# Whole float32 key sums and numerators, and third tiles in the room they leave

## The chip, the cores and the metric

The program runs on one core of a Trainium2 chip. Time is device time of one execution in microseconds (us). The kernel before took 961.89 us in the median of three runs (961.02 to 962.08). A core has five engines: TensorE multiplies matrices (PE in the profile; PEld is its weight load), VectorE (DVE), ScalarE (ACT) and GpSimd (POOL) work on elements, and SyncE (SP) issues most DMAs. Each has its own queue and works through it in order; they meet by semaphores. TensorE writes to PSUM, from which VectorE and ScalarE read.

## The reference

Three layers follow each other. In numpy, with what matters here:

```
def phi(x):                                    # x: q or k, scaled; [4, 8, 576, 64]
    h = einsum(x, omega) - sum(x*x)/2          # 128 features
    return exp(h - max(h)) / sqrt(128)
kv  = einsum('bhsm,bhsd->bhmd', k_p, v);  z = sum(k_p, axis=2)        # key sums
num = einsum('bhsm,bhmd->bhsd', q_p, kv); den = einsum('bhsm,bhm->bhs', q_p, z) + 1e-6
x = (num / den) as [2304, 512]
x = softplus(x @ w_in) @ w_out                 # w_in [512, 2048], w_out [2048, 512], given as float64
x = expert layer: one of 8 experts for each token by cosine, relu(x @ w1[e]) @ w2[e] times its gate
```

The key sums `kv` and `z` are sums over the 576 positions of products of key features and values; a column of ones beside the 64 columns of `v` gives `z` from the same product.

## The kernel before, in words

**Two forms of product.** A matrix product here is either whole, with both operands in float32, or split: each operand is a part rounded to the float32r type (`hi`) and the remainder (`lo`), and hi·hi, hi·lo and lo·hi are summed in PSUM. A split product is three matmuls, and somebody has to make the parts: a cast (VectorE, ScalarE or GpSimd) and a subtraction (VectorE or GpSimd).

**Attention.** The work is cut by batch `b` (4) and head quadruple `u` (2 for each batch; called a head pair below, since each holds two pairs of heads `i`). For each, keys come in four full tiles `w` = (i, half) of 128 partitions x 2 heads x 2 rows, and one short tile `"rem"` for the last 64 positions; queries alike. One tile is an item, and an item is a chain of stages that sit in numbered steps: transpose at step t (`stage_T`), features at t+1 (`stage_P`: products, maximum, exponential), for keys the splitting at t+3 (`stage_S`, with `split_v` for the value tile) and the key sum at t+4 (`stage_K`, on PSUM bank `kv`), then `stage_Z`, which transposes the sums into `kzh` (and the remainder `kzl`). Query features are transposed at t+3 (`stage_Q`, into `qT..hi` and `qT..lo`), and `stage_N` makes numerator and denominator, 256 or 320 columns each. `f_k` and `f_n` in TUNE say for which of the eight head pairs a form is whole: key sums of the full tiles for the first three (`11100000`), numerators for the first four (`11110000`). Short key tiles are split everywhere. A whole key tile needs its values beside a column of ones in float32, so `split_v` copies them (L249) into such a tile and GpSimd sets the ones (L284).

**Loads.** SP loads key, query and value tiles four steps ahead of the item. `raw` and `rawv` have two buffers each, so a load waits for the reader of the tile two before.

**Feed-forward layer.** 2304 tokens are six groups `g` of 384, and the 2048 hidden features 16 chunks `f`; `n` = 16 g + f counts chunks. For a chunk `mm1` makes `h` (one PSUM bank in groups 0 to 3), ScalarE and VectorE make softplus from it (`r` and `t`, L690 to L711), `act_tail` splits it into `gh` and `gl` (L717 to L720), and `mm2` sums into three PSUM banks. `mm1` of chunk n+2 is issued before `mm2` of chunk n. `r`, `gh` and `gl` have two tiles, `t` one. In group 0 all products are whole, later ones split, with weights split anew for each chunk (`ring_in`, `ring_out`).

**Weights.** The two weight matrices come as float64. `load_w` brings a piece of 512 KB as pairs of integers into a staging tile (`wst`, two of them), and `conv_ops` makes float32 of it in three VectorE instructions (L601, L604, L607). `conv_all` loads piece n+1 and then converts piece n; there are 32 pieces.

**What sets the order.** The program emits 30 steps of the attention, then the chunks; between the products of a chunk `attn_point` emits attention stages and one instruction of the conversion by a budget, and a table `need` says which step has to be done before a group starts. The framework then lays out the instructions anew: at build time a planner simulates the engines with costs of its own and takes, on each engine, what is ready first by its reckoning, with the order of emission as priority. The order on the chip is the one that it left, fixed in each engine's queue. Only the expert layer, from its second unit on, keeps a written order.

**Memory.** The attention's tiles lie in pools `ac`, `ap` and `ap1`, which are closed during group 4; the feed-forward layer's lie in `fp`, `ring`, `xpool`, `stg`. A tile of a pool is given out again when its readers are done.

Of the kernel before, what the change touches and what calls it, by code (L numbers as in the profile page):

```python
# [23 lines left out]
    f_k='11100000',  # L24
    f_n='11110000',
# [6 lines left out]
    vf='vvvvvvvv',  # L32
    exp_k='vaaavaaa',
    exp_q='vavvaavv',
    kh='vavvavav',
    kl='ppppvvvv',
    vh='vpvvvvpv',
    vl='ppvppppp',
# [16 lines left out]
    s_lag=3,  # L55
    k_lag=4,
    q_lag=3,
    setup=2,
# [6 lines left out]
    order='XSMTNnKPZ',  # L65
    se={'T': 't', 'Q': '12', 'P': 'p0', 'N0': 'h', 'N1': '12'},
    sl={'T': 't', 'Q': 't', 'P': 'p', 'N0': 't', 'N1': 't'},
    b_vh=3,
# [7 lines left out]
    b_rawv=2,  # L76
# [7 lines left out]
def tile_kernel(ctx, tc, q, k, v, omega, w_in, w_out, emb, tau, w1, w2, out):  # L84
# [94 lines left out]
    raw = {}  # L179

    def load_half(kind, b, j, half):
        src = {"q": q, "k": k, "v": v}[kind]
        nb = TUNE["b_rawv" if kind == "v" else "b_raw"]
        t = atile([P, 2, 2, D], F32, "rawv" if kind == "v" else "raw", b, nb)
        s = src[b, 2 * j:2 * j + 2, 0:S0, :].rearrange("h (p r) d -> p h r d", r=4)
        nc.sync.dma_start(out=t, in_=s[:, :, 2 * half:2 * half + 2, :])
        raw[kind, b, j, half] = t

    def load_rem(kind, b, u):
        src = {"q": q, "k": k, "v": v}[kind]  # L190
        t = ap.tile([P, 2, D], F32, tag="rem", bufs=TUNE["b_rem"], name=f"rem_{kind}_{b}_{u}")
        for i in range(2):
            j = 2 * u + i
            nc.sync.dma_start(
                out=t[SR * i:SR * i + SR],
                in_=src[b, 2 * j:2 * j + 2, S0:S, :].rearrange("h p d -> p h d"))
        raw[kind, b, u, "rem"] = t
# [4 lines left out]
    vhi = [ac.tile([P, 2, 2, D + 1], F32R, name=f"vhi{i}") for i in range(TUNE["b_vh"])]  # L202

    vhr = [ac.tile([P, 2, D + 1], F32R, name=f"vhr{i}") for i in range(2)]
    vlr = [ac.tile([P, 2, D], F32R, name=f"vlr{i}") for i in range(2)]

    def setup():
        obd = stg.tile([P, 2, M], F32, tag="wst", name="obd")
        nc.gpsimd.memset(obd, 0.0)
        for t in vhi:  # L210
            nc.gpsimd.memset(t[:, :, :, D:D + 1].bitcast(F32), 1.0)
        for i in range(2):
            nc.gpsimd.memset(vhr[i].bitcast(F32), 0.0)
            nc.gpsimd.memset(vlr[i].bitcast(F32), 0.0)
            nc.gpsimd.memset(vhr[i][SR * i:SR * i + SR, :, D:D + 1].bitcast(F32), 1.0)
        pt = psum("T", "om_ps")
        nc.tensor.transpose(pt[:, 0:P], om2.rearrange("m j d -> m (j d)"), ident)
        for j in range(2):
            r = slice(64 * j, 64 * j + 64)
            nc.scalar.activation(out=obd[r, j, :], in_=pt[r, 0:P], func=AF.Copy, scale=SC)  # L220
        nc.gpsimd.tensor_copy(obd_hi, obd)
        nc.gpsimd.tensor_tensor(out=obd_lo, in0=obd, in1=obd_hi.bitcast(F32), op=ALU.subtract)
# [14 lines left out]
    def cols(w):  # L237
        return 1 if w == "rem" else 2
# [30 lines left out]
    nv, nk = [0], [0]  # L269

    def split_v(it):
        b, u, kind, w = it
        if w == "rem":
            vr = raw["v", b, u, "rem"]
            for i in range(2):
                r = slice(SR * i, SR * i + SR)
                nc.vector.tensor_copy(vhr[i][r, :, 0:D], vr[r])
                nc.gpsimd.tensor_tensor(out=vlr[i][r], in0=vr[r], in1=vhr[i][r, :, 0:D].bitcast(F32),
                                        op=ALU.subtract)
        else:  # L280
            vr = raw["v", b, 2 * u + w[0], w[1]]
            if kind == "k" and whole("k", b, u):
                vf = atile([P, 2, 2, D + 1], F32, "vl", b)
                nc.gpsimd.memset(vf[:, :, :, D:D + 1], 1.0)  # L284
                move("vf", b, u, vf[:, :, :, 0:D], vr)
                st["v", b, 2 * u + w[0], w[1]] = (vf, None)
                return
            vh = vhi[nv[0] % len(vhi)]
            nv[0] += 1
            vl = atile([P, 2, 2, D], F32R, "vl", b)  # L290
            eng("vh", b, u).tensor_copy(vh[:, :, :, 0:D], vr)
            eng("vl", b, u).tensor_tensor(out=vl, in0=vr, in1=vh[:, :, :, 0:D].bitcast(F32), op=ALU.subtract)
            st["v", b, 2 * u + w[0], w[1]] = (vh, vl)

    def stage_P(it):
# [14 lines left out]
        if kind == "k" and w != "rem" and whole("k", b, u):  # L310
            nk[0] += 1
            pe = atile([P, 4, M], F32, ("kh", "kl")[nk[0] % 2], b)
        else:
            pe = atile([P, 4, M], F32, "pe", b, TUNE["b_pe"])
# [10 lines left out]
    def stage_S(it):  # L325
        b, u, kind, w = it
        n = cols(w)
        pe = st.pop((it, "P"))
        split_v(it)
        if kind == "k" and w != "rem" and whole("k", b, u):  # L330
            st[it, "P"] = (pe, None)
        elif kind == "k":
            kh = atile([P, 4, M], F32R, "kh", b)
            kl = atile([P, 4, M], F32R, "kl", b)
            if TUNE["kh"][2 * b + u] == "a":
                nc.scalar.copy(out=kh[:, :2 * n], in_=pe[:, :2 * n])
            else:
                eng("kh", b, u).tensor_copy(kh[:, :2 * n], pe[:, :2 * n])
            eng("kl", b, u).tensor_tensor(out=kl[:, :2 * n], in0=pe[:, :2 * n],
                                          in1=kh[:, :2 * n].bitcast(F32), op=ALU.subtract)  # L340
            st[it, "P"] = (kh, kl)

    def stage_K(it):
        b, u, kind, w = it
        kh, kl = st.pop((it, "P"))
        if w == (0, 0):
            st["kv", b, u] = psum("kv", "kv")
        kv = st["kv", b, u]
        if w == "rem":
            lst = [(i, h, vhr[i][:, h, :], vlr[i][:, h, :], h) for i in range(2) for h in range(2)]  # L350
        else:
            vh, vl = st.pop(("v", b, 2 * u + w[0], w[1]))
            lst = [(w[0], h, vh[:, h, r, :], None if vl is None else vl[:, h, r, :], 2 * h + r)
                   for r in range(2) for h in range(2)]
        for n, (i, h, a_hi, a_lo, c) in enumerate(lst):
            col = (2 * i + h) * M
            first = w == (0, 0) and n == 0
            o = kv[0:D + 1, col:col + M]
            if kl is None:
                nc.tensor.matmul(o, lhsT=a_hi, rhs=kh[:, c, :], start=first, stop=False, skip_group_check=True)  # L360
                continue
            nc.tensor.matmul(o, lhsT=a_hi, rhs=kh[:, c, :], start=first, stop=False, skip_group_check=True)
            nc.tensor.matmul(o, lhsT=a_hi, rhs=kl[:, c, :], start=False, stop=False, skip_group_check=True)
            nc.tensor.matmul(kv[0:D, col:col + M], lhsT=a_lo, rhs=kh[:, c, :], start=False,
                             stop=(w == "rem"), skip_group_check=True)
        if w == "rem":
            kvs = ap1.tile([D + 1, 512], F32, tag="kvs", name="kvs")
            move("kvs", b, u, kvs, kv[0:D + 1, :])
            st["kvs", b, u] = kvs
# [131 lines left out]
    def add_item(t, it):  # L501
        b, u, kind, w = it
        tl = max(0, t - AHEAD)
        for kd in ("k", "v") if kind == "k" else ("q",):
            if w == "rem":
                loads[tl].append(lambda kd=kd: load_rem(kd, b, u))
            else:
                loads[tl].append(lambda kd=kd: load_half(kd, b, 2 * u + w[0], w[1]))
        steps[t].append(("T", 214, lambda: stage_T(it)))
        steps[t + 1].append(("P", 654, lambda: stage_P(it)))  # L510
        if kind == "k":
            steps[t + TUNE["s_lag"]].append(("S", 0, lambda: stage_S(it)))
            steps[t + TUNE["k_lag"]].append(("K", 648, lambda: stage_K(it)))
            if w == "rem":
                steps[t + TUNE["k_lag"] + 1].append(("Z", 216, lambda: stage_Z(b, u)))
        else:
            steps[t + TUNE["q_lag"]].append(("K", 428, lambda: stage_Q(it)))
# [57 lines left out]
    def load_w(n):  # L575
        f, which = divmod(n, 2)
        t = stg.tile([P, 2 * DM], I32, tag="wst", name="wst")
# [36 lines left out]
    def conv_all():  # L614
        load_w(0)
        for n in range(NW):
            if n + 1 < NW:
                load_w(n + 1)
            yield from conv_ops(n)
            done_w[0] = n + 1  # L620
# [35 lines left out]

    def mm1(n, rate):
# [20 lines left out]

        if two:
            r = fp.tile([P, G], F32, tag="r", name="r")  # L680
# [7 lines left out]
        t = fp.tile([P, G], F32, tag="t", name="t", bufs=1)  # L688
        r = fp.tile([P, G], F32, tag="r", name="r")
# [11 lines left out]
    def act_tail(n):  # L701
        r, t = gt[n]
        if n < NF:
            gf = fp.tile([P, G], F32, tag="gh", name="gf")
# [9 lines left out]
        gh = fp.tile([P, G], F32R, tag="gh", name="gh")  # L714
        gl = fp.tile([P, G], F32R, tag="gl", name="gl")
# [911 lines left out]
```

## Time and profile before

| | us |
|---|---|
| median of the runs (range) | 961.89 (961.02 to 962.08) |
| profiled execution | 964.16 |
| its span, first to last instruction | 962.4 |
| PE busy | 898.1 (93%) |
| DVE busy | 745.9 (78%) |
| ACT busy | 655.6 (68%) |
| POOL busy | 365.4 (38%) |
| mean granted TensorE clock | 0.991 |

The profile shows one execution. Busy time of an engine is the time covered by at least one of its instructions; matmuls overlap, since each is shown with its latency, so the distance from one start to the next tells what a matmul holds the engine for. A name before `<-` is the tile written, the names behind it are read; L303 is a line of the kernel. The first feed-forward product starts at 75.7 us, group 1 at 194.8, group 2 at 309.5, group 3 at 411.7, group 4 at 502.2; the last key sum is at 422.8 and the last numerator at 489.6; the expert layer's products run from 642.6 to 947.9.

### The profile page before, as it was taken

What the parts mean: (1) busy time and instruction counts of PE and PEld (TensorE: products, weight loads), DVE (VectorE), ACT (ScalarE), POOL (GpSimd) and SP (SyncE); (2) the same over time, 40 slices, a digit from 0 to 9 for tenths busy, and PEclk for the clock granted to TensorE, in tenths of its full rate; (3) what the DMA queues carried; (4) which work ended last, traced back from release to release, by engine and by line L of the source; (5) the groups of instructions that cost most, each with busy time, mean ns of one, the idle gap of its engine ahead of it and who ended that gap; (6) DMA issues with size and microseconds to landing.
All of it is one profiled execution on the core that took longest, in us unless ns stands there. A gap on an engine that the chain in (4) does not pass through costs nothing. (4 is left out here: it accounts for less than half of the span.)

```text
span 962.4 us, 15065 instructions
## 1 busy us (share of the span) xinstructions
PE 898.1 (93%) x5095; PEld 744.4 (77%) x5095; DVE 745.9 (78%) x1497; ACT 655.6 (68%) x1463; POOL 365.4 (38%) x396
## 2 busy tenths in 40 slices
PE   7788998999997989999999999999999999999994
PEld 6666554587887978898878899887787888878873
DVE  7999788478997789989997677768976675675762
ACT  4887434477766976777767778777866576585672
POOL 2436302165653676468663210011252252241410
PEclk9999999999999999999999999999999999999997
DMA  5554354011252114011210174101122761551810
GB/s 147 163 150 131 118 188 146 12 31 45 55 125 60 45 36 119 9 35 35 46 26 17 34 269 169 34 12 41 26 78 102 306 234 34 204 185 60 339 65 7
DMA packets 77840, 94.73 MB, mean 98 GB/s; under 512 B 33398, under 2 KB 66166, under 8 KB 75456
## 3 DMA queue, kind: packets, MB, share of 16 engines
q1 hardware_dynamic: 69184, 45.21, 17.7%
q0 software_dynamic: 8576, 48.52, 13.4%
q8 instruction: 42, 0.69, 0.3%
q14 instruction: 38, 0.31, 0.1%
HBM read 108.36 MB, written 15.48 MB: 129 GB/s over the span
## 5 line engine op out<-in xcount | busy, mean ns | idle before, releaser
L1407 PE MATMUL po<-w,mh_h 128*128 128x512 f32 x368 | 116.8, 398 | 0.5 <-ACT mh_h L1384 0.5
L740 PE MATMUL y<-woh,gh 128*128 128x512 f32 x240 | 96.3, 410 | 8.1 <-DVE gh L719 7.6
L1287 DVE TENSOR_TENSOR w<-w2r,w 128x512 fp32r<-128x512 f32 x136 | 88.2, 684 | 14.1 <-ACT w L1283 13.9
L1422 POOL DMA_INDIRECT out_dram<-ot,s_idx x23 | 31.1, 1352 | 170.1 <-ACT ot L1421 139.8
L740 PE MATMUL y<-wol,gh 128*128 128x512 f32 x240 | 93.4, 397 | 0.0
L1283 ACT CAST w<-w2r 128x512 fp32r<-128x512 f32 x136 | 79.4, 643 | 20.6 <-DMA w2r<-in_moe_w_dram,w_idx 7.1
L1287 DVE TENSOR_TENSOR w<-w1r,w 128x1024 fp32r<-128x1024 f32 x68 | 80.4, 1225 | 11.2 <-ACT w L1283 11.1
L640 DVE TENSOR_TENSOR wil<-win,wih 128x512 fp32r<-128x512 f32 x72 | 63.3, 879 | 24.9 <-ACT wih L639 24.5
L740 PE MATMUL y<-woh,gl 128*128 128x512 f32 x240 | 79.4, 400 | 0.0
L1407 PEld LDWEIGHTS po<-w,mh_h 128*128 128x128 f32 x368 | 66.1, 189 | 12.2 <-ACT mh_h L1384 0.7
L1283 ACT CAST w<-w1r 128x1024 fp32r<-128x1024 f32 x68 | 72.0, 1119 | 3.4 <-PE ph L1373 2.1
L1395 PE MATMUL ph<-mxh,w 128*128 128x256 f32 x384 | 73.0, 286 | 1.3 <-DVE w L1287 0.5
L674 PE MATMUL h<-xhi,wih 128*128 128x384 f32 x320 | 72.6, 347 | 1.5 <-DVE t L694 1.3
L1407 PE MATMUL po<-w,mh_l 128*128 128x512 f32 x184 | 72.7, 395 | 0.7 <-DVE mh_l L1386 0.7
L674 PE MATMUL h<-xlo,wih 128*128 128x384 f32 x320 | 69.7, 336 | 0.0
L674 PE MATMUL h<-xhi,wil 128*128 128x384 f32 x320 | 69.7, 337 | 0.0
L652 POOL TENSOR_TENSOR wol<-wout,woh 128x512 fp32r<-128x512 f32 x40 | 58.4, 1460 | 25.7 <-ACT woh L651 18.3
L1395 PEld LDWEIGHTS ph<-mxh,w 128*128 128x128 f32 x384 | 62.7, 195 | 5.1 <-DVE w L1287 3.7
L674 PEld LDWEIGHTS h<-xhi,wih 128*128 128x128 f32 x320 | 55.4, 188 | 6.6 <-DVE t L694 1.8
L740 PEld LDWEIGHTS y<-woh,gh 128*128 128x128 f32 x240 | 45.0, 189 | 18.6 <-DVE gh L719 9.3
L674 PEld LDWEIGHTS h<-xhi,wil 128*128 128x128 f32 x320 | 57.4, 188 | 0.0
L1260 POOL DMA_INDIRECT w1r<-in_moe_w_dram,w_idx x17 | 22.5, 1324 | 91.2 <-issue 55.8
(346 smaller groups left out, 2588.9 us busy)
## 6 DMA issues: line engine op xcount, KB each, us to landing
wst<-in_moe_w_in_dram SPq DMA_DIRECT2D x16, 512.0 KB, 3.9
wst<-in_moe_w_out_dram SPq DMA_DIRECT2D x16, 512.0 KB, 3.6
raw<-in_k_dram SPq DMA_DIRECT2D x32, 128.0 KB, 2.4
rawv<-in_v_dram SPq DMA_DIRECT2D x32, 128.0 KB, 2.3
raw<-in_q_dram SPq DMA_DIRECT2D x32, 128.0 KB, 2.2
ya<-yt SPq DMA_DIRECT2D x20, 128.2 KB, 4.9
yb<-yt SPq DMA_DIRECT2D x20, 128.2 KB, 3.7
ya<-yt SPq DMA_DIRECT2D x8, 256.5 KB, 5.0
```

Source lines behind the costliest of these rows:

```text
L640: feng("il", n).tensor_tensor(out=il, in0=wi, in1=ih.bitcast(F32), op=ALU.subtract)
L652: feng("ol", n).tensor_tensor(out=ol, in0=wo, in1=oh.bitcast(F32), op=ALU.subtract)
L674: nc.tensor.matmul(h[:, 0:G], lhsT=a[:, c, :], rhs=x[:, c, :], start=(i == 0), stop=(i == last))
L740: nc.tensor.matmul(y, lhsT=x[:, c], rhs=w, start=(f == 0 and i == 0), stop=(f == NF - 1 and i == len(passes) - 1))
L1260: nc.gpsimd.indirect_dma_start(out=raw_w[nm, s % 2], out_offset=None, in_=src, in_offset=bass.IndirectOffsetOnAxis(ap=w_idx[:, s:s + 1].bi ...
L1283: nc.scalar.copy(out=hi, in_=src)
L1287: eng.tensor_tensor(out=lo, in0=src, in1=hi.bitcast(F32), op=ALU.subtract)
L1395: nc.tensor.matmul(ph[:, j * 256:j * 256 + 256], lhsT=w1s[g, c][b_][:, f], rhs=xs[g][a][c].rearrange("p i t -> p (i t)"), start=(c == 0 an ...
L1407: nc.tensor.matmul(po[s], lhsT=h[a][:, o:o + P], rhs=w2s[g, c][b_], start=(c == 0 and n == 0), stop=(c == 7 and n == 2))
L1422: nc.gpsimd.indirect_dma_start(out=out, out_offset=bass.IndirectOffsetOnAxis(ap=s_idx[:, s:s + 1].bitcast(U32), axis=0), in_=ot, in_offset ...
```

## The change

All key sums, of the short tiles too, and all numerators become whole products. `stage_S` and `split_v` go, and with them the tiles `vhi`, `vhr`, `vlr`, `vl`, `rawv` and, unused now, `kzl` and `qT..lo`. The features go straight from `stage_P` into `stage_K`, in the four buffers that `kh` and `kl` had. Values are loaded by DMA straight into one of six tiles `vf` (short ones into `vfr`) whose column of ones is set once, two DMAs for a full tile, placed one step ahead of the item instead of four. Every third piece of the weights is staged in a third tile `wst3`, and loads go out two pieces ahead. In groups 0 to 3 every third chunk takes `r`, `gh` and `gl` from a third tile, and `t` has two.

```diff
-    f_k='11100000',
-    f_n='11110000',
+    f_n='11111111',
-    s_lag=3,
+    v_ahead=1,
-    b_vh=3,
+    b_vf=6,
-    b_rawv=2,
...
     def load_half(kind, b, j, half):
+        if kind == "v":
+            t = vf[nv[0] % len(vf)]
+            nv[0] += 1
+            for h in range(2):
+                nc.sync.dma_start(out=t[:, h, :, 0:D], in_=s[:, h, 2 * half:2 * half + 2, :])
+        else:
+            t = atile([P, 2, 2, D], F32, "raw", b, TUNE["b_raw"])
+            nc.sync.dma_start(out=t, in_=s[:, :, 2 * half:2 * half + 2, :])
...
     def load_rem(kind, b, u):
+            if kind == "v":
+                nc.sync.dma_start(
+                    out=vfr[u][i][SR * i:SR * i + SR, :, 0:D],
+                    in_=src[b, 2 * j:2 * j + 2, S0:S, :].rearrange("h p d -> p h d"))
+                continue
...
+    vf = [ac.tile([P, 2, 2, D + 1], F32, name=f"vf{i}") for i in range(TUNE["b_vf"])]
+    vfr = [[ac.tile([P, 2, D + 1], F32, name=f"vfr{n}{i}") for i in range(2)] for n in range(2)]
...
-        if kind == "k" and w != "rem" and whole("k", b, u):
+        if kind == "k":
             nk[0] += 1
             pe = atile([P, 4, M], F32, ("kh", "kl")[nk[0] % 2], b)
...
-    def stage_S(it):
...
     def stage_K(it):
+        if w == "rem":
+            lst = [(i, h, vfr[u][i][:, h, :], h) for i in range(2) for h in range(2)]
+        else:
+            vr = raw["v", b, 2 * u + w[0], w[1]]
+            lst = [(w[0], h, vr[:, h, r, :], 2 * h + r) for r in range(2) for h in range(2)]
+        for n, (i, h, a, c) in enumerate(lst):
             col = (2 * i + h) * M
+            nc.tensor.matmul(kv[0:D + 1, col:col + M], lhsT=a, rhs=pe[:, c, :], start=w == (0, 0) and n == 0,
+                             stop=w == "rem", skip_group_check=True)
...
-                loads[tl].append(lambda kd=kd: load_half(kd, b, 2 * u + w[0], w[1]))
+                tv = max(0, t - TUNE["v_ahead"]) if kd == "v" else tl
+                loads[tv].append(lambda kd=kd: load_half(kd, b, 2 * u + w[0], w[1]))
...
     def load_w(n):
         f, which = divmod(n, 2)
-        t = stg.tile([P, 2 * DM], I32, tag="wst", name="wst")
+        if n % 3 == 2:
+            t = ap1.tile([P, 2 * DM], I32, tag="wst3", name="wst3")
+        else:
+            t = stg.tile([P, 2 * DM], I32, tag="wst", name="wst")
...
         load_w(0)
+        load_w(1)
         for n in range(NW):
-            if n + 1 < NW:
-                load_w(n + 1)
+            if n + 2 < NW:
+                load_w(n + 2)
...
+    def chain(n, tag, dt, name):
+        if n // NF < LATE and n % 3 == 2:
+            return ap1.tile([P, G], dt, tag=f"{tag}3", name=name)
+        return fp.tile([P, G], dt, tag=tag, name=name)
...
+        r = chain(n, "r", F32, "r")
...
-        t = fp.tile([P, G], F32, tag="t", name="t", bufs=1)
-        r = fp.tile([P, G], F32, tag="r", name="r")
+        t = ap1.tile([P, G], F32, tag="t", name="t", bufs=2)
...
-        gh = fp.tile([P, G], F32R, tag="gh", name="gh")
-        gl = fp.tile([P, G], F32R, tag="gl", name="gl")
+        gh = chain(n, "gh", F32R, "gh")
+        gl = chain(n, "gl", F32R, "gl")
```

## Rows read from the trace of the kernel before

**Rows 1.** Busy by stage: PE, PEld, DVE, ACT, POOL; clock, DMA share, GB/s
```profile
25.00:76.00 51.00, 41.02 (x265) 32.52 (x264) 49.85 (x99) 43.49 (x134) 22.49 (x31) 0.97 0.53 156
76.00:175.00 99.00, 90.02 (x390) 54.43 (x390) 80.48 (x171) 47.47 (x128) 27.22 (x38) 1.00 0.44 136
...
197.00:502.20 305.20, 287.66 (x1834) 254.62 (x1833) 270.81 (x512) 227.00 (x577) 192.69 (x191) 0.99 0.22 53
502.20:962.40 460.20, 438.51 (x2404) 373.27 (x2402) 318.14 (x655) 316.27 (x577) 113.17 (x94) 0.99 0.33 116
```

**Rows 2.** TensorE's waits, 197 to 502.2: us in total, times, longest
```profile
PE y L740 <- DVE gh L719: 7.6, 9, 2.8
PE nd L441 <- DVE qT1lo L428: 2.7, 1, 2.7
```

**Rows 3.** TensorE's waits, 76 to 175
```profile
PE h L674 <- DVE t L694: 2.5, 2, 1.3
...
PE kv L362 <- DVE kh L338: 1.3, 2, 0.9
```

**Rows 4.** Timeline of TensorE around key sums: start, us, what, count
```profile
13.79 1.04 PE L360 MATMUL kv<-kh,vl 128*65 128x128 f32 x8
14.66 0.38 PE L261 MATMUL pt_q<-ident,raw 128*128 128x128 f32 x2
...
283.66 0.22 PE L363 MATMUL kv<-kl,vhi 128*65 128x128 f32 x1
...
284.26 0.22 PE L364 MATMUL kv<-kh,vl 128*64 128x128 f32 x1
```

**Rows 5.** Timeline of TensorE around numerators: whole, whole, split
```profile
63.13 1.03 PE L441 MATMUL nd<-qT0hi,kzh 128*128 128x256 f32 x4
64.00 1.05 PE L360 MATMUL kv<-kl,vl 128*65 128x128 f32 x6
...
176.80 0.70 PE L441 MATMUL nd<-qT1hi,kzh 128*128 128x320 f32 x2
177.34 0.38 PE L411 MATMUL pt_q<-ident,pe 128*128 128x128 f32 x2
...
279.17 0.32 PE L441 MATMUL nd<-qT1hi,kzh 128*128 128x320 f32 x1
...
279.61 0.69 PE L674 MATMUL h<-xhi,wil 128*128 128x384 f32 x3
```

**Rows 6.** Groups of TensorE, 197 to 502.2: count, busy us, mean ns
```profile
L363 PE MATMUL kv<-kl,vhi 128*65 128x128 f32 x64 | 13.2, 231 | 0.0
...
L363 PE MATMUL kv<-kl,vhr 128*65 128x128 f32 x16 | 3.2, 226 | 0.0
```

**Rows 7.** Groups of VectorE, 197 to 502.2; the last row 25 to 76
```profile
L339 DVE TENSOR_TENSOR kl<-pe,kh 128x512 fp32r<-128x512 f32 (+1 forms) x20 | 17.3, 865 | 0.1
L428 DVE TENSOR_TENSOR qT0lo<-pt_q,qT0hi 128x512 fp32r<-128x512 f32 x8 | 5.4, 673 | 0.5 <-ACT qT0hi L247 0.5
L428 DVE TENSOR_TENSOR qT1lo<-pt_q,qT1hi 128x512 fp32r<-128x512 f32 x8 | 5.3, 667 | 0.0
L338 DVE CAST kh<-pe 128x512 fp32r<-128x512 f32 (+1 forms) x10 | 5.0, 505 | 1.2 <-ACT pe L321 1.2
...
L249 DVE COPY vl<-rawv 128x256 f32<-128x256 f32 x6 | 3.0, 496 | 0.1
```

**Rows 8.** VectorE's waits, 76 to 175
```profile
DVE win L601 <- DMA wst<-in_moe_w_in_dram: 6.5, 7, 2.4
DVE wout L601 <- DMA wst<-in_moe_w_out_dram: 6.2, 8, 1.8
```

**Rows 9.** The page's DMA issues: count, size of one, us to landing
```profile
wst<-in_moe_w_out_dram SPq DMA_DIRECT2D x16, 512.0 KB, 3.6
```

**Rows 10.** Timeline of SP, 289 to 292
```profile
289.34 1.07 SPq L186 DMA_DIRECT2D rawv<-in_v_dram  x2
```

**Rows 11.** SP's waits, 0 to 76
```profile
SPq L186 <- PE pt_k L261: 8.9, 6, 2.7
```

More of the change, by code (lines that the diff above doesn't have):

```diff
@@ L31 @@
     qt='vvaaaaaa',
-    vf='vvvvvvvv',
     exp_k='vaaavaaa',
     exp_q='vavvaavv',
[L35 to L38, printed above, removed]
     xl='pppppppp',
@@ L64 @@
     man=1,
-    order='XSMTNnKPZ',
+    order='XMTNnKPZ',
     se={'T': 't', 'Q': '12', 'P': 'p0', 'N0': 'h', 'N1': '12'},
     sl={'T': 't', 'Q': 't', 'P': 'p', 'N0': 't', 'N1': 't'},
-    b_vh=3,
+    b_vf=6,
     yb='pppp',
@@ L179, in tile_kernel @@
     raw = {}
+    nv, nk = [0], [0]
     def load_half(kind, b, j, half):
         src = {"q": q, "k": k, "v": v}[kind]
-        nb = TUNE["b_rawv" if kind == "v" else "b_raw"]
-        t = atile([P, 2, 2, D], F32, "rawv" if kind == "v" else "raw", b, nb)
         s = src[b, 2 * j:2 * j + 2, 0:S0, :].rearrange("h (p r) d -> p h r d", r=4)
-        nc.sync.dma_start(out=t, in_=s[:, :, 2 * half:2 * half + 2, :])
+        if kind == "v":
[6 more added lines that the diff above has]
+            nc.sync.dma_start(out=t, in_=s[:, :, 2 * half:2 * half + 2, :])
         raw[kind, b, j, half] = t
@@ L190, in load_rem @@
         src = {"q": q, "k": k, "v": v}[kind]
-        t = ap.tile([P, 2, D], F32, tag="rem", bufs=TUNE["b_rem"], name=f"rem_{kind}_{b}_{u}")
+        t = None if kind == "v" else \
+            ap.tile([P, 2, D], F32, tag="rem", bufs=TUNE["b_rem"], name=f"rem_{kind}_{b}_{u}")
         for i in range(2):
             j = 2 * u + i
+            if kind == "v":
[3 more added lines that the diff above has]
+                continue
             nc.sync.dma_start(
@@ L201, in tile_kernel @@
     obd_lo = ac.tile([P, 2, M], F32R, name="obd_lo")
-    vhi = [ac.tile([P, 2, 2, D + 1], F32R, name=f"vhi{i}") for i in range(TUNE["b_vh"])]
-    vhr = [ac.tile([P, 2, D + 1], F32R, name=f"vhr{i}") for i in range(2)]
-    vlr = [ac.tile([P, 2, D], F32R, name=f"vlr{i}") for i in range(2)]
+    vf = [ac.tile([P, 2, 2, D + 1], F32, name=f"vf{i}") for i in range(TUNE["b_vf"])]
+    vfr = [[ac.tile([P, 2, D + 1], F32, name=f"vfr{n}{i}") for i in range(2)] for n in range(2)]
     def setup():
@@ L209, in setup @@
         nc.gpsimd.memset(obd, 0.0)
[L210 to L215, printed above, removed]
+        for t in vf:
+            nc.gpsimd.memset(t[:, :, :, D:D + 1], 1.0)
+        for t2 in vfr:
+            for i in range(2):
+                nc.gpsimd.memset(t2[i], 0.0)
+                nc.gpsimd.memset(t2[i][SR * i:SR * i + SR, :, D:D + 1], 1.0)
         pt = psum("T", "om_ps")
@@ L267, in stage_T @@
         st[it, "T"] = (hi, lo)
[L269 to L293, printed above, removed]
     def stage_P(it):
@@ L323, in stage_P @@
         st[it, "P"] = pe
-    def stage_S(it):
[L326 to L341, printed above, removed]
     def stage_K(it):
         b, u, kind, w = it
-        kh, kl = st.pop((it, "P"))
+        pe = st.pop((it, "P"))
         if w == (0, 0):
@@ L349, in stage_K @@
         if w == "rem":
-            lst = [(i, h, vhr[i][:, h, :], vlr[i][:, h, :], h) for i in range(2) for h in range(2)]
+            lst = [(i, h, vfr[u][i][:, h, :], h) for i in range(2) for h in range(2)]
         else:
[L352 to L355, printed above, removed]
+            vr = raw["v", b, 2 * u + w[0], w[1]]
+            lst = [(w[0], h, vr[:, h, r, :], 2 * h + r) for r in range(2) for h in range(2)]
+        for n, (i, h, a, c) in enumerate(lst):
             col = (2 * i + h) * M
[L357 to L365, printed above, removed]
+            nc.tensor.matmul(kv[0:D + 1, col:col + M], lhsT=a, rhs=pe[:, c, :], start=w == (0, 0) and n == 0,
+                             stop=w == "rem", skip_group_check=True)
         if w == "rem":
@@ L511, in add_item @@
         if kind == "k":
-            steps[t + TUNE["s_lag"]].append(("S", 0, lambda: stage_S(it)))
             steps[t + TUNE["k_lag"]].append(("K", 648, lambda: stage_K(it)))
@@ L687, in mm1 @@
             return
-        t = fp.tile([P, G], F32, tag="t", name="t", bufs=1)
-        r = fp.tile([P, G], F32, tag="r", name="r")
+        t = ap1.tile([P, G], F32, tag="t", name="t", bufs=2)
         nc.scalar.activation(out=r, in_=h[:, 0:G], func=AF.Relu)
@@ L703, in act_tail @@
         if n < NF:
-            gf = fp.tile([P, G], F32, tag="gh", name="gf")
+            gf = chain(n, "gh", F32, "gf")
             nc.vector.tensor_tensor(out=gf, in0=r, in1=t, op=ALU.add)
```

## The prediction, made before the result was known

> **What bounds the kernel now.** I read the table by stage first. The attention's lead-in (25 to 76 us) is VectorE's: it works 49.85 of 51 us, TensorE 41.0 [rows 1]. From 76 us the feed-forward chunks run and TensorE takes over: 90.0 of 99 us up to 175, 287.7 of 305.2 from 197 to 502, with VectorE close behind (270.8 of 305.2). After 502 us no attention is left; the change edits nothing there, and TensorE is at 438.5 of 460.2. So up to 502 us two engines share the limit: products that become cheaper count whole between 76 and 502, and VectorE's work counts before 76 and wherever TensorE stands for it.
>
> The list of waits says for whom it stands. From 197 to 502 the rows leave 17.5 us without a product; 7.6 of these are output products waiting for the rounded activation `gh` and 2.7 one wait for a query remainder [rows 2]. From 76 to 175 us the rest is 9.0, with 2.5 for `t` (the one bank of `h` is not read out yet) and 1.3 for a key cast [rows 3]. These waits end on VectorE, in whose queue the attention's splits stand between the chunk's steps.
>
> **Part 1: the products.** What counts is the distance between starts, since the durations overlap. A split key product issues every 0.60/10 = 60 ns (283.66 to 284.26 us, ten distances), so a triple holds TensorE 180 ns. The whole form stands in the trace too, on the first three head pairs: eight in a row, and the next entry, a transpose, starts 0.87 us after the first of them: 109 ns each [rows 4]. A triple made whole gives back 71 ns. There are 5 head pairs x 16 full-tile triples + 8 x 4 of the short tiles = 112: 80 of them after 197 us [rows 6], 24 in the first feed-forward group (the short tile of the third pair and all of the fourth), 8 in the lead-in. That is 80 x 71 = 5.7 us, 24 x 71 = 1.7 us, and 0.6 us where VectorE is the limit, which I count as nothing: its cover is VectorE's 97.7%, and if that cover goes it is 0.6 more.
>
> Numerators: a split one of 320 columns takes 0.44 us until the next product starts (279.17 to 279.61); two whole ones take 0.54, 0.27 each: 0.17 saved. A split one of 256 columns, at the same time per column, takes 0.35; four whole ones take 0.87, 0.22 each: 0.13 saved [rows 5]. Four head pairs x 8 products, half of either size: 16 x 0.17 + 16 x 0.13 = 4.8 us, all in the stretch from 197. So TensorE's work falls by 1.7 us between 76 and 197 and by 10.5 after.
>
> By the Trainium skill, FP8 and Floating Point Precision, section TensorE Precision Notes, a true FP32 product makes four passes through the array. By it the part would lose 11 us (the last rival) where the rows make it a gain of 12; the trace disagrees, with 109 ns for a whole product against 60 for a rounded one, 1.8 passes and not four [rows 4].
>
> **Part 2: VectorE and GpSimd.** Between 197 and 502 us VectorE loses the key remainders (17.3), two groups of query remainders (5.4, 5.3) and key casts (5.0): 33.0 of its 270.8 us, with smaller groups beside [rows 7]. It would be busy 238 of some 288 us: its idle share goes from 11% to 17%. What of TensorE's 17.5 us does this give back? The 2.7 us wait is on an instruction that is gone. Of the others the bounds are 0 and all of the 14.8. I take 4.8, a third: the same rows after 502 us, where no attention stands in VectorE's queue, still leave TensorE 4.7% of the span idle, so the rest does not vanish. That gives 7.5 us, bounds 0 and 17.5 (and below 0 if the new order makes new waits, see the rivals).
>
> Before 76 us the copies of the whole value tiles go, 3.0 us between 25 and 76 [rows 7]; VectorE is the limit there, so I count 3.0 (bounds 0, if the conversion of the weights is only drawn forward into the gap, and 5, an estimate: the short tiles' casts go as well, fewer and smaller than these). ScalarE, next in line, is at 43.5 of 51 us, which hides no more than that.
>
> **Part 3: third staging tile, loads two ahead.** The conversion of the weights runs with two staging tiles: a load goes out when the tile two back is converted, lands 3.6 us later [rows 9], and VectorE waits at the head of its queue: 12.7 us in 15 waits between 76 and 175 us [rows 8]. With a third tile the load leaves one conversion earlier, about the landing time sooner, which covers every one of these waits (the longest is 2.4 us). But they are VectorE's, not TensorE's: of TensorE's 9.0 us there, 1.3 is for a key cast that goes, and I add half of the 2.5 for `t`: with VectorE no longer held at the head of its queue, the step that reads `h` out comes sooner. 2.5 us; bounds 0 and 9.0. The DMA engines are at 0.44 in this stage, so the third load finds room.
>
> **Part 4: third `r`, `gh`, `gl`, second `t`.** They let the chunk's elementwise chain start before the products two chunks back are done. The waits they could end are those of part 2 ([rows 2, 3]); I count nothing twice. A third tile cannot end the wait for `h`, since its bank stays single.
>
> **Part 5: the values' loads.** Each full value half is now two DMAs, each some 0.53 us of SP's queue [rows 10]: 32 more issues, 17 us over 400 us. I cost them at nothing, since the load has five steps of other work to hide behind: it is placed one step ahead of the item and the product that reads it comes four steps after it (before, two buffers bound the load and the split came after three). The upper bound is the slow rival's. The ones column is set once by GpSimd instead of before each whole tile, off the path in both.
>
> **Sum.** 3.0 (lead-in) + 1.7 + 2.5 (first group) + 10.5 + 7.5 (the three groups after it) = 25.2 us. The profiled execution took 964.16 us (its span 962.4 and 1.8 around it), so 939.0; the median of the runs shown, 961.89, is 2.3 lower than that execution, so 936.7: I say **937**.
>
> **Rivals.**
> - *Products only.* The freed time of VectorE stays idle: the new order leaves as many waits, and the lead-in is filled up with conversion. Then 1.7 + 10.5 = 12.2: 949.7. For it: TensorE's idle time is small change in many places (9 waits for `gh`); against it: one of the named waits is on a removed instruction.
> - *All of it.* Every idle microsecond in the rows comes back: 5 + 1.7 + 9.0 + 10.5 + 17.5 = 43.7: 918. Against it: 4.7% idle after 502.
> - *Slower: value loads hold TensorE.* The key products now wait for a DMA themselves, in TensorE's own queue, and all products behind them wait too. In the lead-in a step is 76/30 = 2.5 us, so five steps are 12.7 us, and the load stands on SP behind key and query loads that wait for their buffers: 8.9 us in six waits, the longest 2.7, on key transposes alone [rows 11]. If each of the 12 full and 3 short value tiles there came 2.7 us late, TensorE would stand 40 us: 964.2 + 40 - 25 - 2 = 977. It decides from 25/15 = 1.7 us lateness per tile. Against it: five steps are longer than any wait shown.
> - *Given back.* The order is laid anew by a planner. Standstills like the longest one for `gh` (2.8 us) at nine new places eat the 25: 962, no change.
> - *Four passes.* With 240 ns for 180, and a third more for each numerator (0.15 and 0.12 us), 112 x 0.06 + 16 x 0.15 + 16 x 0.12 = 11 us are lost on TensorE, with the 13 us of the other parts kept (3.0 + 2.5 + 7.5): 962 less 2.3 is 960, no change within what can be told. The spacing of the whole products in the trace leaves little of it. It is the rule of the page named in part 1.
>
> **How the numbers follow.** A run of this kernel can be told from no change at about 0.2%, 1.9 us. Forecast 0.61 (its own range 927 to 947); products only 0.16; all of it 0.08; slower 0.08; given back 0.05; four passes 0.02. Faster: 0.61 + 0.16 + 0.08, and 0.01 of the given-back case, 0.86; same 0.06; slower 0.08. The range from 919 to 955 takes in products only with 5 us of new waits, and nearly all of the full gain; it leaves out the slow case, the two without change, and some 0.03 of the ends: 0.18.
>
> **What would show it.** Right: the starts of the key products 109 ns apart in all groups, the numerators 0.21 and 0.27 us; VectorE's waits for `wst` between 76 and 175 us near zero; the first chunk 3 us earlier; the stretch from the second group's first product to the last attention product 18 us shorter, with TensorE idle near 10 us in it; after that the same 460 us. Wrong: key products ended by a DMA of `v`; a first chunk that starts later; a stretch after the attention that is longer; TensorE's idle time in the three groups still at 17 us.

## The result and the profile after

The changed kernel took 951.25 us (median of four runs, 950.67 to 953.13) where the one before took 961.99 (four runs): a ratio of 0.9867, 95% interval 0.9838 to 0.9896. Its profiled execution took 950.99 us, span 949.1, granted clock 0.991 as before. The forecast was 937, in a range of 919 to 955. So the direction and the range held, the size did not, and the reason for the size is a step that had the wrong sign.

Busy time by stage (PE, PEld, DVE, ACT, POOL, clock, DMA share, GB/s), which answers to [rows 1]; the last numerator is at 480.9 us, and the third stretch runs on to 490, 3.2 us into group 4:

```profile
25.00:76.00 51.00, 40.24 (x254) 32.10 (x254) 42.84 (x84) 42.26 (x131) 20.03 (x20) 0.97 0.66 190
76.00:175.00 99.00, 92.84 (x375) 56.05 (x374) 73.59 (x157) 49.43 (x129) 18.21 (x24) 1.00 0.43 129
197.00:490.00 293.00, 283.73 (x1707) 251.38 (x1706) 232.66 (x431) 220.94 (x562) 169.70 (x164) 0.99 0.23 53
490.00:949.10 459.10, 436.81 (x2397) 372.10 (x2395) 317.07 (x648) 315.25 (x576) 127.42 (x93) 0.99 0.33 116
```

VectorE fell as worked out (232.7 of 293 us against 270.8 of 305.2), GpSimd too. TensorE is now without a product for 9.3 us of the long stretch, where it was 17.5; up to the first product of group 4 it is 7.6. What the table cannot show is how much work lies under "busy". The groups of TensorE over the whole run can (count, busy us, mean ns):

```profile
L318 PE MATMUL kv<-kh,vf 128*65 128x128 f32 x128 | 20.5, 283 | 0.8 <-ACT kh L301 0.6
L318 PE MATMUL kv<-kl,vf 128*65 128x128 f32 x128 | 19.7, 277 | 0.0
...
L395 PE MATMUL nd<-qT1hi,kzh 128*128 128x320 f32 x64 | 22.4, 441 | 4.8 <-ACT xf L252 2.0 <-ACT kh L301 2.0 <-DVE qT1hi L254 0.8
...
L395 PE MATMUL nd<-qT0hi,kzh 128*128 128x256 f32 x64 | 18.5, 380 | 0.0
```

The program asks for 8 head pairs x 4 full tiles x 4 = 128 key products from full tiles and 8 x 8 = 64 numerators. The trace has 256 and 128. **A whole product is two instructions.** The spacing itself is as forecast, 0.87/8 = 109 ns:

```profile
346.11 1.03 PE L318 MATMUL kv<-kl,vf 128*65 128x128 f32 x8
346.98 1.04 PE L318 MATMUL kv<-kh,vf 128*65 128x128 f32 x8
```

But eight of these are four products, one tile. A whole key product holds TensorE for 218 ns, a split one for 180; a whole numerator 0.54 or 0.44 us against 0.44 or 0.35. TensorE's work did not fall by 12.2 us but rose by 112 x 38 ns + 16 x 0.10 + 16 x 0.08 us = 7.1.

To set work against standstill I counted each matmul of both traces with its distance from start to start (one rounded product: 60, 118, 146, 174, 230 ns for 128, 256, 320, 384, 512 columns; one instruction of a whole one: 109, 216, 269, 322, 429), with transposes of 128 columns at 109 as well, summed by stage, and took the rest as time without work. What a product takes longer at the lower granted clock falls into the rest too; up to group 4 the clock stood at 0.50 for 6.8 us in both kernels (half of it in the lead-in, half in group 1 before and in group 2 after), so it does not make the difference of the sums. The stages are bounded by the first product of each feed-forward group:

| stage | before: us = products + rest | after: us = products + rest |
|---|---|---|
| lead-in | 75.7 = 47.3 + 28.4 | 74.0 = 46.7 + 27.3 |
| group 0 | 119.1 = 104.9 + 14.1 | 115.5 = 105.8 + 9.8 |
| group 1 | 114.7 = 97.2 + 17.5 | 99.6 = 97.5 + 2.2 |
| group 2 | 102.2 = 92.8 + 9.4 | 104.8 = 97.9 + 7.0 |
| group 3 | 90.5 = 84.1 + 6.4 | 92.8 = 85.9 + 6.9 |
| group 4 to the end | 460.2 | 462.3 |

Up to group 4 products rise by 7.5 us (the 7.1 within the count's error) and the rest falls by 22.6. Group 1 gains most, groups 2 and 3 get longer. Why it is group 1 is not shown: VectorE was busy for 86% of it before (98.1 of 114.7 us) and for 96% of group 3 (86.5 of 90.5).

TensorE's waits of the long stretch, to set against [rows 2] (us in total, times, longest):

```profile
PE y L703 <- DVE gh L682: 3.2, 4, 1.4
PE h L638 <- DVE t L657: 2.5, 3, 1.7
PE nd L395 <- ACT xf L252: 2.0, 1, 2.0
```

The waits for `gh` fell from 7.6 to 3.2 and the one on a query remainder is gone; the longest wait for `t` lies in group 4 already, at 489.3 us. No key product waits for a load of values. The waits of VectorE for staged weights, against [rows 8], are 9.3 us in 10 where they were 12.7 in 15:

```profile
DVE wout L558 <- DMA wst<-in_moe_w_out_dram: 6.5, 6, 2.7
DVE win L558 <- DMA wst<-in_moe_w_in_dram: 2.8, 4, 1.0
```

### The profile page after: what moved, and what is told of

It reads as the page before. It is cut to its first block, busy times and chain, and to the rows that moved or that the text cites. A ratio compares the mean times of both kernels' runs of the same rounds, so it can differ in the third digit from the quotient of the medians.

```text
span 949.1 us, 14505 instructions
## 1 busy us (share of the span) xinstructions
PE 895.0 (94%) x4951; PEld 743.6 (78%) x4951; DVE 694.6 (73%) x1376; ACT 651.7 (69%) x1452; POOL 345.1 (36%) x341
## 5 line engine op out<-in xcount | busy, mean ns | idle before, releaser
L1385 POOL DMA_INDIRECT out_dram<-ot,s_idx x23 | 46.3, 2015 | 166.9 <-ACT ot L1384 126.0
L703 PE MATMUL y<-woh,gl 128*128 128x512 f32 x240 | 81.5, 406 | 0.4 <-POOL gl L683 0.4
L598 DVE TENSOR_TENSOR wil<-win,wih 128x512 fp32r<-128x512 f32 x72 | 56.9, 790 | 29.2 <-ACT wih L597 25.9
L1370 PEld LDWEIGHTS po<-w,mh_h 128*128 128x128 f32 x368 | 66.1, 189 | 12.2 <-ACT mh_h L1347 0.7
L425 POOL TENSOR_TENSOR xf<-xf,rc 128x256 f32<-128x256 f32 (+1 forms) x20 | 19.9, 994 | 143.7 <-ACT rc L424 129.0
L638 PE MATMUL h<-xlo,wih 128*128 128x384 f32 x320 | 71.9, 340 | 0.0
L610 POOL TENSOR_TENSOR wol<-wout,woh 128x512 fp32r<-128x512 f32 x40 | 54.2, 1355 | 27.8 <-ACT woh L609 24.9
L638 PEld LDWEIGHTS h<-xlo,wih 128*128 128x128 f32 x320 | 56.5, 188 | 0.5
```

The lines of the kernel that those rows point to most:

```text
L425: nc.gpsimd.tensor_tensor(out=xf, in0=xf, in1=rc, op=ALU.mult)
L598: feng("il", n).tensor_tensor(out=il, in0=wi, in1=ih.bitcast(F32), op=ALU.subtract)
L610: feng("ol", n).tensor_tensor(out=ol, in0=wo, in1=oh.bitcast(F32), op=ALU.subtract)
L638: nc.tensor.matmul(h[:, 0:G], lhsT=a[:, c, :], rhs=x[:, c, :], start=(i == 0), stop=(i == last))
L703: nc.tensor.matmul(y, lhsT=x[:, c], rhs=w, start=(f == 0 and i == 0), stop=(f == NF - 1 and i == len(passes) - 1))
L1370: nc.tensor.matmul(po[s], lhsT=h[a][:, o:o + P], rhs=w2s[g, c][b_], start=(c == 0 and n == 0), stop=(c == 7 and n == 2))
```

## The experiments

Two accounts were set against each other. **A:** the gain is relief: the splits leave VectorE's and GpSimd's queues, TensorE stands less, and pays 7 us for it. **B:** the third tiles give the gain, and the whole products only make room and cost. Times are medians of six runs (e6 five, e7 and e8 twelve) beside the kernel before on the same chip, whose median there was 962.3 to 964.7; behind each median stands the ratio to it, with its 95% interval. The kernel after was not run again beside them: differences to it are differences of medians, and by the ratios they come out up to 2.5 us otherwise.

**e1, no third tile.**

```diff
-        if n // NF < LATE and n % 3 == 2:
+        if False:
...
-        t = ap1.tile([P, G], F32, tag="t", name="t", bufs=2)
+        t = ap1.tile([P, G], F32, tag="t", name="t", bufs=1)
...
-        if n % 3 == 2:
-            t = ap1.tile([P, 2 * DM], I32, tag="wst3", name="wst3")
...
-            if n + 2 < NW:
-                load_w(n + 2)
+            if n + 1 < NW:
+                load_w(n + 1)
```

> The kernel after without any third tile: two staging tiles with loads one piece ahead, two r, gh, gl and one t. Theory A (the gain is VectorE's and GpSimd's relief: the splits are gone from their queues, and TensorE stands less; the whole products themselves cost TensorE some 7 us, since each is two instructions of 109 ns): 950 to 954 us, nearly all of the gain stays, and TensorE's idle time between the first feed-forward product and group 4 stays near that of the kernel after. Rival B (the gain comes from the third tiles, the whole products only make room and cost): 962 to 969, the kernel before plus what the products cost.

954.2 us, 0.9912 (0.9883 to 0.9940). A, just outside its range: most of the gain stands without a third tile. Group 4 even starts earlier, at 484.8 us against 486.8; what e1 loses lies behind that (467.1 us to the end against 462.3), where a block of comparisons holds VectorE's queue, as e8 and e9 show.

**e2, without the chain's third tiles** (the first two edits of e1 alone).

> The kernel after without the third r, gh, gl and the second t, with the third staging tile kept. Theory A: 950 to 954, no change that can be told from the kernel after. Rival B, if the chain's tiles are what pays: 957 to 965, with TensorE's waits for gh and for the reader of h back at 10 us or more in groups 1 to 3.

951.47 us, 0.9881 (0.9851 to 0.9910): the same as the kernel after, so A holds.

**e3, without the third staging tile** (the last two edits of e1 alone).

> The kernel after with two staging tiles and loads one piece ahead, the chain's third tiles kept. Theory A: 950 to 954. Rival B, if staging is what pays: 955 to 960, the first feed-forward group 4 us or more longer (it took 115.5 us after and 119.1 before), since VectorE's waits for the staged weights grow from 9 to 13 us or more.

952.7 us, 0.9907 (0.9875 to 0.9939): by the time A holds. Group 0 did get longer, 121.9 us against 115.5, with VectorE's waits for staged weights at 19.0 us, as B said, and group 1 took 5.3 us more; but group 0 started 2.6 us earlier and groups 2 and 3 took 6.8 us less. Group 4 starts 2.2 us later: most of what the staging tile gives at first is given back.

**e4, third tiles with split keys.** The kernel before with the chain and staging edits of the change, and:

```diff
-    f_n='11110000',
+    f_n='11111111',
```

> The kernel before with whole numerators and all third tiles, but key sums split as before (whole only in the full tiles of the first three head pairs; the values' loads and copies as before). Theory A: VectorE has the key splits back (25 us of casts and remainders), TensorE saves 112 x 38 ns = 4 us: 955 to 962. Rival B: all room is in use and TensorE's work is smaller, 945 to 951, faster than the kernel after.

972.89 us, 1.0102 (1.0070 to 1.0134), slower than the kernel before. B falls, and A's own range, no slower than before, is missed by 11 us. TensorE's rest up to group 4 is 82.0 us (75.8 before), and the granted clock averaged 0.982 in place of 0.991: up to group 4 it stood at 0.50 for 24 us in place of 6.8. At half speed that is up to 8.5 us more, an estimate, so the clock alone can account for the 6.2 us by which the rest rose. Whole numerators alone do no such harm (e7), so third tiles without the relief do, in this order; which of their waits did it was not separated.

**e5, VectorE's share put back.** In `stage_K` of the kernel after:

```diff
+        if 2 * b + u >= 3 and w != "rem":
+            dm = ap1.tile([P, 4, M], F32R, tag="dm", name="dm")
+            nc.vector.tensor_copy(dm, pe)
+            nc.vector.tensor_tensor(out=dm, in0=pe, in1=dm.bitcast(F32), op=ALU.subtract)
```

> The kernel after, with VectorE's part of the key split put back as dead work: for each of the 20 full key tiles from the fourth head pair on, a cast and a subtraction of 128x512 into a tile that nobody reads (some 20 x 1.2 = 24 us of VectorE). The products stay whole and wait for none of it. Theory A1 (the gain is VectorE's time: its queue is shorter, so the chunk's steps that TensorE waits for come sooner): 957 to 964, TensorE's idle time in groups 1 and 2 up by 6 us or more. Rival A2 (the gain is the shorter path from features to key sum, GpSimd's relief and the values' loads, not VectorE's time): 950 to 954.

958.14 us, 0.9939 (0.9920 to 0.9957): 6.9 us over the kernel after, for dead work that nothing waits for. Its groups on VectorE add up to 27.3 us:

```profile
L311 DVE TENSOR_TENSOR dm<-kh,dm 128x512 fp32r<-128x512 f32 x10 | 8.7, 870 | 0.2
L311 DVE TENSOR_TENSOR dm<-kl,dm 128x512 fp32r<-128x512 f32 x10 | 7.8, 779 | 0.1
L310 DVE CAST dm<-kl 128x512 fp32r<-128x512 f32 x10 | 6.0, 600 | 3.7 <-ACT kl L301 3.0 <-ACT kl L298 0.7
L310 DVE CAST dm<-kh 128x512 fp32r<-128x512 f32 x10 | 4.8, 480 | 0.2 <-ACT kh L298 0.2
```

No instruction of the trace waits for `dm`. So VectorE's queue is a cause (A1). The dead work takes back 6.9 of the 22.6 us; the rest of the relief, be it GpSimd's, the shorter path to the key sum or the values' loads, was not taken apart. TensorE's rest in groups 1 and 2 rose by 3.9 us, less than the 6 that A1 named.

**e6, every key product twice.**

```diff
+            for j in range(2):
+                nc.tensor.matmul(kv[0:D + 1, col:col + M], lhsT=a, rhs=pe[:, c, :],
+                                 start=w == (0, 0) and n == 0 and j == 0, stop=w == "rem" and j == 1, skip_group_check=True)
```

> The kernel after with every key product issued twice into the same sum (key sums and normaliser are both doubled, so the quotient stays but for the epsilon): 160 more whole products of two instructions of 109 ns, 34.9 us of TensorE and nothing else. Theory (TensorE's work counts whole from the first feed-forward product on, 126 of the 160 products, and little before): 976 to 986. Rival (TensorE has slack where the attention runs, since VectorE shares the limit): below 968; then the 7 us that whole products cost in the kernel after would also be mostly hidden.

986.64 us, 1.0229 (1.0208 to 1.0250): 35.4 us over the kernel after and just above the range. Its groups show 256 + 256 and 64 + 64 instructions:

```profile
L319 PE MATMUL kv<-kl,vf 128*65 128x128 f32 x256 | 33.7, 273 | 1.8 <-ACT kl L301 1.8
L319 PE MATMUL kv<-kh,vf 128*65 128x128 f32 x256 | 33.1, 272 | 0.0
L319 PE MATMUL kv<-kh,vfr 128*65 128x128 f32 x64 | 8.6, 274 | 0.5 <-ACT kh L301 0.5
L319 PE MATMUL kv<-kl,vfr 128*65 128x128 f32 x64 | 8.0, 273 | 0.0
```

160 products more at 218 ns are 34.9 us, but the nearness to 35.4 is in part luck. In groups 0 to 3 stand 112 more products, 24.4 us at 218 ns and 12.2 at 109: these groups got 25.7 us longer (438.5 against 412.8), of which up to 3.4, an estimate, are due to 6.8 us more at a granted clock of 0.50. That is far from 12.2 even so: it prices a whole product by time, and TensorE's work counts nearly whole there, so the 7 us, nearly all of which stand in these groups, are really paid. The lead-in holds the other 48 products, 10.5 us, and got 5.0 longer (79.0 against 74.0): there a part is hidden. The last 4.9 us lie from group 4 on (467.2 against 462.3), where the edit adds nothing; TensorE stands there for 2.78 us behind the comparisons that e8 is about.

**e7, whole numerators alone, and e8, whole keys of the full tiles alone**, each in the kernel before:

```diff
-    f_n='11110000',
+    f_n='11111111',
```

> The kernel before with whole numerators for all eight head pairs and nothing else changed. TensorE does 16 x 78 + 16 x 98 ns = 2.8 us more, VectorE 16 us less (query and key-sum remainders). Theory A: 954 to 960, faster. Rival B (only the third tiles pay): 963 to 966.

965.33 us, 1.0013 (0.9998 to 1.0029): no change; A fails for the numerators.

```diff
-    f_k='11100000',
+    f_k='11111111',
```

> The kernel before with whole key sums in the full tiles of all eight head pairs (short tiles still split, values still copied by VectorE) and nothing else changed. TensorE does 80 x 38 ns = 3 us more, VectorE about 20 us less net of 20 copies of values, GpSimd 20 us less. Theory A: 952 to 959, faster. Rival B: 963 to 967.

960.21 us, 0.9964 (0.9951 to 0.9976), just outside A's range. The stages say more: group 4 starts at 489.8 us, 12.4 earlier than before, most of the change's 15.4. From there to the end it takes 467.2 us, 7.0 more than before; 5.3 of these are group 4 (73.5 against 68.2), and the timeline of VectorE (start, us, what, count) shows where:

```profile
488.98 3.84 DVE L1070 TENSOR_SCALAR am<-iota,pos_all 128x128 bf16<-128x128 bf16 x9
492.74 0.35 DVE L719 CAST gh<-r 128x384 fp32r<-128x384 f32 x1
```

Nine comparisons of the router, ready early, stand in one block ahead of the cast that TensorE needs. Before and in the kernel after, eight of them stand in a block too, but the step behind it is the one that reads out `h`, and TensorE waits 0.53 and 1.65 us for it:

```profile
499.80 3.24 DVE L1070 TENSOR_SCALAR am<-iota,pos_all 128x128 bf16<-128x128 bf16 x8
503.56 0.97 PE L674 MATMUL h<-xhi,wih 128*128 128x384 f32 x4 [0.53 <-DVE t L694]
```
```profile
485.90 2.85 DVE L1033 TENSOR_SCALAR am<-iota,pos_all 128x128 bf16<-128x128 bf16 x8
489.27 0.97 PE L638 MATMUL h<-xhi,wih 128*128 128x384 f32 x4 [1.65 <-DVE t L657]
```

**e9, the block taken apart.** e2 has the same block of nine, as have e1 and e11. VectorE first, then TensorE, then the stage table of the stretch behind it:

```profile
483.48 3.92 DVE L1033 TENSOR_SCALAR am<-iota,pos_all 128x128 bf16<-128x128 bf16 x9
487.32 0.35 DVE L682 CAST gh<-r 128x384 fp32r<-128x384 f32 x1
```
```profile
484.40 0.97 PE L638 MATMUL h<-xhi,wih 128*128 128x384 f32 x4 [0.45 <-ACT wih L597]
487.72 0.79 PE L703 MATMUL y<-woh,gh 128*128 128x512 f32 x1 [2.35 <-DVE gh L682]
488.32 0.63 PE L703 MATMUL y<-wol,gh 128*128 128x512 f32 x1
488.74 0.63 PE L703 MATMUL y<-woh,gh 128*128 128x512 f32 x1
```
```profile
488.30:491.50 3.20, 3.20 (x10) 2.70 (x9) 1.92 (x3) 0.91 (x2) 1.45 (x2) 0.50 0.00 0
```

After the stand of 2.35 us the products come 0.42 us apart in place of 0.23: the granted clock is 0.50, the lower level of 1.2 GHz, and it stays there until 493.5. e9 is e2 with each comparison tied behind the end of a chunk of group 4:

```diff
             act_tail(n + 1)
+            if g == LAST - 1:
+                marks["oh", f] = traced()
...
             for T in range(NT_A):
-                place_onehot(T)
+                with tc.issue_after(marks["oh", 2 + T]):
+                    place_onehot(T)
```

> The kernel of the run without the chain's third tiles, with the nine one-hot comparisons of the router (3.9 us of VectorE in one block, which stood ahead of the cast to gh at the start of group 4 there, followed by 2.35 us without a product and 3.4 us at the granted clock of 0.5) tied one by one behind the ends of chunks 2 to 10 of group 4. Theory (that block is a place where VectorE's queue still holds TensorE, and the low clock behind it costs again): 945 to 949, the group from 484.4 us on 4 to 5 us shorter and no stretch of low clock there. Rival (the stand only moves): 950 to 953.

946.31 us, 0.9819 (0.9793 to 0.9845): the fastest of all, 5.2 us under e2. The same place in it, on TensorE:

```profile
484.14 0.97 PE L638 MATMUL h<-xhi,wih 128*128 128x384 f32 x4 [0.45 <-ACT wih L597]
484.95 0.39 PE L703 MATMUL y<-woh,gh 128*128 128x512 f32 x1
485.18 0.40 PE L703 MATMUL y<-wol,gh 128*128 128x512 f32 x1
```
```profile
484.00:491.00 7.00, 6.86 (x36) 6.37 (x37) 5.39 (x7) 4.24 (x11) 4.91 (x5) 1.00 0.01 2
```

Group 4 and what follows take 461.5 us from its start; in e2 it was 466.6.

**e10, the same tie in the kernel after.**

> The kernel after with the same tie of the nine comparisons. There the block did little harm (group 4 took 69.4 us against 68.2 before): theory 949 to 951, a microsecond at most; if the tie by itself disturbs the order, 952 or more.

948.42 us, 0.9839 (0.9815 to 0.9863), a little better than expected: group 4 went from 69.4 to 67.5 us, and the stand of 1.65 us for `t` is gone. Beside the same runs of the kernel before, e9, without the chain's third tiles, is 2.1 us faster than this one with them, though the two intervals overlap.

**e11, numerators split again.** e1 with `f_n='11110000'`.

> The kernel without any third tile, with numerators split again in the last four head pairs (as before), key sums whole. TensorE saves 2.8 us, VectorE has 16 us of remainders back in groups 1 to 3. If numerators give by VectorE what they cost on TensorE (as the kernel before with whole numerators, no gain, says): 952 to 956, the same as without the third tiles (954.2). If VectorE's relief counts for them as for the keys: 957 to 961. If TensorE's price decides: 950 to 952.

954.43 us, 0.9897 (0.9870 to 0.9925): as e1, with runs from 950.85 to 956.49. With e7 this says that whole numerators give on VectorE what they cost on TensorE, as near as these runs tell.

**e12, another order of the same work.** `rate=139` in place of 140.

> The kernel after with the attention's budget per chunk at 139 instead of 140: the same work, but the planner lays out some hundreds of TensorE's instructions elsewhere. It measures what a new order alone is worth. Theory (orders differ by one or two standstills of 2 to 5 us): 948 to 955. Rival (the order decides as much as the change itself): outside 944 to 959; then none of the differences under 8 us between the other runs tells anything.

951.55 us, 0.9883 (0.9843 to 0.9922). It tells little: by the names and shapes in the traces, TensorE's order differs from the kernel after in 33 of 4951 places, not in some hundreds. What a new order alone is worth stays open. Of the third tiles I read no more than that they are worth some 4 us at most (e1 and e3 by the ratios). In the profiled executions the kernels without the chain's third tiles reach group 4 earlier (e2 484.4, e1 484.8 us) than those with them (486.8, e3 489.0).

## Why the prediction was right, and where it was wrong

- **Part 1 failed.** It read "eight in a row ... 109 ns each" as eight products [rows 4]; they are four, as e6 confirms by time. The list of TensorE's groups in the kernel before had what shows it: group 0 needs 16 x 4 whole products for `h` and has 128 instructions; for the first three head pairs L360 stands twice with 48, for 48 products (rows below this list). The sentence that the trace disagrees with the four passes rests on the same misreading. The term was -12.2 us and is +7.1. The Trainium skill, FP8 and Floating Point Precision, section TensorE Precision Notes, gives four passes for true FP32; 218 ns against 60 is 3.6, which comes near the page's four. I set the rule aside with a number that had its error in it, and gave the rival built on it 0.02. Its price (11 us, at 240 ns) was the nearest to the truth of all terms for the products.
- **Part 2, with part 3's share, had the mechanism and half the size.** The rest in groups 0 to 3 fell by 21.5 us (47.4 to 25.9); I had taken 10.0. A third of the waits that remained was too little. Why more came back is not shown; e5 says only that VectorE's queue holds 6.9 us of it.
- **The lead-in** moved by 1.7 us, not 3.0. The stretch from the first product of group 1 to the last numerator, a sign that was to be 18 us shorter, is 3.4 shorter (291.4 us against 294.8), with the four groups as in the table.
- **Part 3 failed in small.** The waits for staged weights did not go to near zero (9.3 us); e3, where they are 19.0, is 1.5 us slower by the medians, so they set little of the time.
- **Part 4 and part 5 held.** e2 is as fast without the chain's third tiles; no key product waits for a value load, so the slow rival's mechanism did not appear.
- **From group 4 on** I had nothing; it is 2.1 us longer, with the stand of 1.65 us behind the block of comparisons. In e10, where they are tied, the same stretch takes 460.0 us.
- **A slip in a rival.** With four passes, 13.0 less 11.0 is 2.0 and not 2.3; its time of 960 stays.

The rows of the kernel before that part 1 had overlooked:

```profile
L674 PE MATMUL h<-x,win 128*128 128x384 f32 x128 | 44.9, 491 | 2.6 <-DVE t L694 2.5
...
L360 PE MATMUL kv<-kh,vl 128*65 128x128 f32 x48 | 7.6, 282 | 1.6 <-ACT kh L321 1.6
L360 PE MATMUL kv<-kl,vl 128*65 128x128 f32 x48 | 7.2, 273 | 0.0
```

The sum: -25.2 forecast for the profiled execution, -13.2 measured, as +7.5 (products), -1.1 (rest of the lead-in), -21.5 and +2.1 (rounding of the parts leaves 0.2). That the time lies inside the range is luck in part: two errors of opposite sign left it there, near the rival "products only" (949.7), whose account of it is the opposite of what happened.

One stand of the new order, in group 2, shows what is left. The timeline of TensorE, then the stretch behind the stand:

```profile
350.04 0.81 PE L395 MATMUL nd<-qT1hi,kzh 128*128 128x320 f32 x2 [2.03 <-ACT xf L252]
350.69 1.19 PE L318 MATMUL kv<-kl,vf 128*65 128x128 f32 x8
...
352.10 0.63 PE L703 MATMUL y<-wol,gh 128*128 128x512 f32 x1
352.52 0.63 PE L703 MATMUL y<-woh,gl 128*128 128x512 f32 x1
```
```profile
351.50:354.80 3.30, 3.30 (x11) 2.62 (x9) 1.93 (x8) 2.77 (x9) 1.46 (x2) 0.50 0.18 68
```

A numerator waits 2.03 us for ScalarE to read out the bank, and behind it the clock is at its lower level again. Chunk 9 of group 2 takes 13.2 us (342.7 to 355.9), about twice its neighbours.

## What to carry to other kernels

Before a spacing becomes a price, count: instructions in the trace against products in the program. A product may be several instructions, and the group's count shows it. Where two engines share the limit, it can pay to give the engine that is nearly full 7 us more if that takes 38 off the queue that it waits for (VectorE's busy time in the long stretch); try the parts singly, since here whole keys carried the gain, whole numerators gave nothing, and third tiles did harm without the relief. Then look for what the new order puts at the head of a queue: one block of nine small comparisons cost 5.2 us, about half of the 10.7 us that the whole change gained.

## What the runs showed that was not expected

- A block of 3.9 us in VectorE's queue cost 5.2 us of time (e2 against e9), more than its length. The stand is 2.35 us, and behind it TensorE ran for 5.8 us (487.7 to 493.5) at a granted clock of 0.50; half of these, 2.9 us as an estimate, make up the rest.
- Some of VectorE's instructions got shorter: the weight remainder of 128x512 up to group 4 took 982 ns on the mean before and 823 after (41 of them each). GpSimd was busy for 169.7 us of 293 in the long stretch in place of 192.7 of 305.2; whether that is the reason was not tested.
- Extra work for TensorE in the lead-in, where it had 28 of 76 us free, still counted by half: 5.0 us for 10.5 (e6).
- The same few comparisons cost TensorE 0.53 us in one order and more than 5 in another, by which step of the chunk stood behind them.
